# Turning the last batch's queries and keys by DMA, with half of the first folds on GpSimd and PSUM banks chosen by the plan

## Chip, cores and metric

One Trainium2 chip, one core. The metric is the device time of one launch in microseconds, the median of several runs. Line numbers (L351) are those of the kernel before in its profile.

## What is computed

Two layers after each other, for 4 batches, 8 heads of 64, 768 positions. First, attention in chunks of 32 queries: each chunk sees 16 keys to its left, its own 32, 8 to its right, and 8 memory keys. The heads side by side are `x` of 768 x 512. Then:

```
X = np.fft.fft(x, axis=1)
X = np.fft.fft(X, axis=2)
u = x + np.real(X)
mu, var = mean and variance of u over its last axis
un = (u - mu) / np.sqrt(var + 1e-06)
out = u + np.maximum(un @ w_ch1, 0.0) @ w_ch2       # 512 -> 2048 -> 512
```

## The kernel before

**Attention** works on pairs of heads, `n = 0..15`, four for each batch. GpSimd issues the loads of queries and keys (`e_load_qk`, L324), cast to bf16, with eight consecutive positions in a partition: `qs` and `ks` are 96 partitions x 2 heads x 512, three buffers each. TensorE turns them (`turn`, L351: 16 transposes for each tile into the PSUM bank `tr`), ScalarE copies the queries out (`e_qT`, L360) and puts the keys with their overlap into `kTb` (`e_kT`, L379; VectorE in batch 0). Twelve tiles of 64 queries against 128 keys follow in two groups: scores (`e_scores`, L392), exp (`e_exp`, L400), values (`e_values`, L416), and the division on VectorE (`e_norm`, L426 and L427) into `xsb`. The values are loaded by SyncE (`e_load_v`, L333 to L342).

**Fourier.** VectorE folds `xsb` by its symmetries (`e_zy`, `e_pq`, `e_ff`; in batch 0 `g_zy` L556 and `g_ff` L569 to L574, in halves `g` as the rows come). ScalarE and VectorE split each fold into two fp16 parts (`e_hi`, `e_lo`, `g_hi` L590, `g_lo` L594). TensorE multiplies with cosine and sine tables along the rows (`e_rows` L488, `g_row` L614, `g_rows` L627), ScalarE and VectorE split again (L500, L505), TensorE goes along the columns (`e_columns` L638). In batches 1 to 3 the second half of the rows is written to DRAM (GpSimd, L522), mirrored there (SyncE, L526 and L527) and loaded again (GpSimd, L531).

**MLP.** Statistics and centring (L652, L658), then the turn of `un`: on TensorE in batch 0, by DMA transposes on SyncE in the others (`e_flip`, L670). `e_ch1` (L698) and `e_relu` (L706) make `hT`, `e_ch2` (L713) and `e_osb` (L720) the output, in two halves of the positions for each batch. PSUM banks for these come from two pools, `acc` and `mlp`, two banks each.

**The order** on each engine is written out by a planner, `Plan`. Every task has an engine, a cost, what it comes after, tags it takes and gives (buffers and banks), a rank, and for a DMA `moved` (its time alone on the DMA engines) and `late` (what is added until it lands). `order` plays this forward and places on each engine the first task in rank that is ready. MLP tasks have the highest ranks and fill TensorE's gaps. On the chip each engine then takes its instructions in that order and waits for what is missing. `share` divides the DMA engines between the queues. On GpSimd a rank below that of the loads puts a task ahead of them. `behind` holds a task back until another has been issued. For some 33 us TensorE's gaps are filled with matmuls on zeros (`e_fill`, L771).

The loads of pair n stand behind those of pair n - 1, and the first pair of batch 1 behind a one-element copy (`gate`, L824) that waits for the values of the last pair of batch 0:

```
lq, lk = [add("POOL", 0.9, lambda i=i: e_load_qk(n, i), take=(("qs", "ks")[i],),
              moved=1.2, late=LATE if b else 0.0,
              behind=t_gate if n == HP else t_ck.get(n - 1), ...
```

Of the kernel before, what the change touches and what calls it, by code (L numbers as in the profile page):

```python
# [36 lines left out]
class Plan:  # L37
# [11 lines left out]
    def __init__(self, slots):  # L49
        self.free = dict(slots)  # L50
        self.tasks = []

    def add(self, engine, cost, emit, after=(), take=(), give=(), rank=None, moved=0.0,
            loose=False, late=0.0, filler=False, behind=None, lag=0.0):
# [3 lines left out]
                 late=late, filler=filler, behind=behind, lag=lag)  # L58
# [3 lines left out]
    def share(self, now):  # L62
# [3 lines left out]
        while any(left.values()):  # L66
            heads = [xs_[0] + [2.0 if q == "POOL" else 1.0] for q, xs_ in left.items() if xs_]
            live = [h for h in heads if h[2] <= at + 1e-9]
            whole = sum(h[3] for h in live)
            step = min([h[1] * whole / h[3] for h in live]  # L70
# [4 lines left out]
            for q, xs_ in left.items():  # L75
                if xs_ and xs_[0][2] <= at - step + 1e-9:
                    xs_[0][1] -= step * (2.0 if q == "POOL" else 1.0) / whole
# [12 lines left out]
    def order(self):  # L90
        now, idle = 0.0, {}
        self.flow, self.seen = {}, 0.0
        waiting = {}
# [6 lines left out]
        while any(waiting.values()):  # L100
            for tag in [g for g in gives if g[0] <= now]:
                gives.remove(tag)
                self.free[tag[1]] += 1
            moved = False
            for e, ts_ in waiting.items():
# [3 lines left out]
                for t in ts_:  # L109
# [12 lines left out]
                    for tag in t["take"]:  # L122
                        need[tag] = need.get(tag, 0) + 1
# [3 lines left out]
                    for tag in t["take"]:  # L127
                        self.free[tag] -= 1
                    cost = t["cost"] * (2.0 if e == "PE" and now < self.WARM else 1.0)
                    idle[e] = t["end"] = now + cost  # L130
                    if t["moved"]:
                        self.flow.setdefault(e, []).append([t, t["moved"], now + cost])
                        self.share(now)
                        t["end"] = t["done"]
                    else:
                        t["done"] = now + cost + self.LAG.get(e, 0.07)
                    for tag in t["give"]:
                        gives.append((t["done"], tag))
# [25 lines left out]
def kernel(  # L164
# [61 lines left out]
    NKT = 2  # L226
    kTb = [spool.tile([P, NT, P], BF16, name=f"kTb{i}") for i in range(NKT)]

    cp_q = "p h j d -> p h (j d)"
# [3 lines left out]
    plan = Plan(dict(qs=NS, ks=NS, va=NV, kTb=NKT, qT=2, tr=1, sc=1, xa=1, e1=3,  # L233
# [87 lines left out]
    def e_load_qk(n, i):  # L321
        b, pr = seq[n]
        src, dst = ((q, qs), (k, ks))[i]
        nc.gpsimd.dma_start(dst[n % NS][0:QP],  # L324
# [28 lines left out]

    def e_turn_q(n):
# [22 lines left out]
    def e_kT(n, eng=None):  # L377
        trk = tr_of.pop((n, 1))
# [6 lines left out]
    def e_scores(n, g):  # L385
        qT, kT = qT_of[n], kTb[n % NKT]
        sc_of[n, g] = sc = aps.tile([P, 2, 8, 64], FP32, tag="sc", bufs=1, name="sc")
        for t6 in range(6):
            t = 6 * g + t6
            for hh in range(2):  # L390
                r0 = 64 * hh
                nc.tensor.matmul(sc[:, hh, t6, :], kT[r0:r0 + 64, t, :],  # L392
                                 qT[r0:r0 + 64, ts(t, 64)], start=True, stop=True,
# [158 lines left out]
    def g_zy(par, g):  # L552
        if g == 0:
            zy_of[0, par] = fpool.tile([P, NST, P], FP32, tag="unT", bufs=2, name="zy0")
        xb, sl = xs[0], slice(3 * g, 3 * g + 3)
        nc.vector.tensor_tensor(zy_of[0, par][:, sl], xb[:, sl, 0:P], xb[:, sl, HD:HD + P],  # L556
                                ALU.add if par == 0 else ALU.subtract)

    def g_ff(par, ab, g, last):
# [3 lines left out]
        zy, ff = zy_of[0, par][:, sl], ff_of[0, par][:, ab, sl]  # L563
        plus = ab == par
        if last:
            plus = plus == (par == 0)
        if not last:
            if ab == 0:
                nc.vector.tensor_copy(ff[:, :, 0], zy[:, :, 0])  # L569
            elif par == 0:  # L570
                nc.vector.memset(ff[:, :, 0:1], 0.0)
        elif (par, ab) == (1, 1):
            nc.vector.tensor_tensor(ff[:, :, 0], xb[:, :, P], xb[:, :, HD + P], ALU.subtract)
        nc.vector.tensor_tensor(ff[:, :, 1:P], (ff if last else zy)[:, :, 1:P],  # L574
# [115 lines left out]
    def mtag(b, i):  # L690
        return "acc" if i % 3 == 2 else "mlp"
# [3 lines left out]
    def e_ch1(b, sh, ht):  # L695
        ph_of[b, sh, ht] = ph = bank(mtag(b, ht), [P, 512], FP32, "ph")
# [12 lines left out]
    def e_ch2(b, sh, stl, part):  # L709
        if part == 0:  # L710
            pc_of[b, sh, stl] = bank(mtag(b, stl), [P, DM], FP32, "pc")
# [95 lines left out]
    t_gate, LATE = None, 1.0  # L807

    def attention(n):
# [3 lines left out]
        lq, lk = [add("POOL", 0.9, lambda i=i: e_load_qk(n, i), take=(("qs", "ks")[i],),  # L813
                      moved=1.2, late=LATE if b else 0.0,
                      behind=t_gate if n == HP else t_ck.get(n - 1),
# [3 lines left out]
                 take=("va",), moved=2.7, late=LATE if b else 0.0)  # L819
        t_lv[n] = lv  # L820
        t_ck[n] = lk
        if n == HP - 1:
            def e_gate():
# [3 lines left out]
        tq = add("PE", 0.40, lambda: e_turn_q(n), [lq, t_idb], take=("tr",), give=("qs",))  # L827
        dve = ("DVE", nc.vector.tensor_copy) if n < HP else ("ACT", None)
        eq = add("ACT", 0.80, lambda: e_qT(n), [tq], take=("qT",), give=("tr",),
                 rank=SINES - 0.5 if n == 0 else None)  # L830
        ktag = "acc" if first else "tr"
        tk = add("PE", 0.43, lambda: e_turn_k(n), [lk, t_idb, t_kz if n == 0 else t_kzs], take=(ktag,), give=("ks",))
        mk = t_mk[n] = add("DVE", 0.2, lambda: e_mkT(n), [t_mkT, t_kTz[n % NKT], t_mk.get(n - 1)],
                           take=("kTb",))
        ek = add(dve[0], 1.25 if dve[1] else 1.04, lambda: e_kT(n, dve[1]), [tk, mk], give=(ktag,))
# [68 lines left out]
    def weights(n):  # L904
        if n == HP + 1:
            t_w1.extend(add("POOL", 0.7, lambda dt=dt: nc.gpsimd.dma_start(
                w1_sb[:, dt, :], moe_w_ch1[ts(dt, P), :]), moved=2.55,
                behind=t_ck[n], rank=t_ck[n]["rank"] + 0.1) for dt in range(NDT))
        else:
            t_w2.extend(add("POOL", 0.7, lambda g=g: nc.gpsimd.dma_start(  # L910
                w2_sb[:, ts(g, 4), :], w2v[:, ts(g, 4), :]), moved=3.1,
                behind=t_ck[n], rank=t_ck[n]["rank"] + 0.1) for g in range(4))

    def first_fourier():
        t_rest, t_mid, t_row, pre = {}, {}, {}, {}
        for g in range(2):
            for par in range(2):
                zy = add("DVE", 0.5, lambda par=par, g=g: g_zy(par, g),
                         [t_norm[0, g], t_norm[1, g], t_sines],
                         take=("unT",) if g == 0 else ())  # L920
                for ab in range(2):
                    pre[par, ab, g] = add("DVE", 0.62 if ab == 0 else 0.5,
                                          lambda par=par, ab=ab, g=g: g_ff(par, ab, g, 0),
                                          [zy, t_norm[2, g]],
# [34 lines left out]
    def fourier(b):  # L959
        t_x1 = add("POOL", 1.0, lambda: e_rows_out(b), [t_norm[b * HP + i, 1] for i in range(HP)],  # L960
                   moved=2.0)
        t_x2[b] = add("SP", 0.6, lambda: e_rows_turn(b), [t_x1], moved=5.5, loose=True)
# [172 lines left out]
```

## Time and profile before

| | us |
|---|---|
| runs | 294.01, 292.42, 291.95 |
| the profiled execution | 292.92 |
| its span | 291.2 |
| TensorE busy | 274.1 |
| VectorE, ScalarE busy | 164.8, 164.9 |
| GpSimd busy | 48.2 |
| L698 and L713, busy | 88.9, 88.0 |
| L416, busy | 25.9 and 3.6 |
| L351, busy | 9.3 and 9.1 |
| L392, busy | 11.4 |

The busy time of a line adds up the time in which any of its instructions was under way. TensorE's matmuls overlap, so the mean of one row (218 ns for L351) times its count is far more than its busy time. The sums of the last batch alone are read from the list in order of time, start to next start. Attention of batch 0 lies at 5 to 32 us, its Fourier part at 33 to 60, the last attention group of batch 3 at about 160, the last Fourier part at 185 to 210, and from there to 287 there are only MLP matmuls on TensorE.

### The profile page before, as it was taken

What the parts mean: (1) busy time and instruction counts of PE and PEld (TensorE: products, weight loads), DVE (VectorE), ACT (ScalarE), POOL (GpSimd) and SP (SyncE); (2) the same over time, 40 slices, a digit from 0 to 9 for tenths busy, and PEclk for the clock granted to TensorE, in tenths of its full rate; (3) what the DMA queues carried; (4) which work ended last, traced back from release to release, by engine and by line L of the source; (5) the groups of instructions that cost most, each with busy time, mean ns of one, the idle gap of its engine ahead of it and who ended that gap; (6) DMA issues with size and microseconds to landing.
All of it is one profiled execution on the core that took longest, in us unless ns stands there. A gap on an engine that the chain in (4) does not pass through costs nothing.

```text
span 291.2 us, 7349 instructions
## 1 busy us (share of the span) xinstructions
PE 274.1 (94%) x3055; PEld 172.7 (59%) x3055; DVE 164.8 (57%) x354; ACT 164.9 (57%) x294; POOL 48.2 (17%) x96
## 2 busy tenths in 40 slices
PE   1589998999999999999999999999899999999994
PEld 1366797765566766566677646656554644545541
DVE  7968997952259874948885878864912012012011
ACT  6896546777566586877885246433750721712700
POOL 8824832220321010221010021010020000000000
PEclk9999999999999999999999999999999999999998
DMA  6998999997999987799952356944222504004204
GB/s 106 194 192 152 201 212 197 197 198 145 174 193 279 173 203 131 102 138 210 184 69 90 37 140 187 146 145 110 54 54 74 108 2 125 21 36 107 39 36 108
DMA packets 98689, 38.36 MB, mean 132 GB/s; under 512 B 85728, under 2 KB 93920, under 8 KB 98656
## 3 DMA queue, kind: packets, MB, share of 16 engines
q1 hardware_dynamic: 87344, 21.83, 40.7%
q0 software_dynamic: 10592, 15.21, 28.4%
q10 hardware_dynamic: 720, 0.85, 0.9%
q8 instruction: 24, 0.39, 0.6%
q14 instruction: 9, 0.07, 0.1%
HBM read 37.36 MB, written 13.37 MB: 174 GB/s over the span
## 4 chain that ended last, share of the span: by engine, by line
PE 86%; POOL 4%; DVE 4%; DMA 2%; ACT 1%; issue 1%; POOLq 0%; DVEq 0%
PE pc L713 29%; PE ph L698 28%; PE xa L416 7%; PE ps L488 5%; PE pm L638 3%; PE sc L392 3%; DMA ks<-in_k_dram 2%; PE ps L627 2%; PE trk L351 2%; PE trq L351 2%; PE idle L771 2%; DVE st L652 1%; DVE xsb L644 1%; POOL qs L324 1%; PE xo L416 1%
## 5 line engine op out<-in xcount | busy, mean ns | idle before, releaser
L706 ACT ACTIVATE hT<-ph 128x384 f16<-128x384 f32 x128 | 60.8, 492 | 53.0 <-PE ph L698 52.0
L698 PE MATMUL ph<-unT,w_sb 128*128 128x384 f16 x512 | 88.9, 327 | 0.9 <-ACT hT L706 0.6
L713 PE MATMUL pc<-w_sb,hT 128*128 128x512 f16 x384 | 88.0, 380 | 0.0
L698 PEld LDWEIGHTS <-w_sb 128*128 128x128 f16 x512 | 48.3, 98 | 33.2 <-issue 1.8
L713 PEld LDWEIGHTS <-hT 128*128 128x128 f16 x384 | 35.8, 98 | 40.6 <-issue 0.4
L720 DVE SCALAR_TENSOR_TENSOR osb<-pc,rstd,xsb 128x512 f32<-128x512 f32 x24 | 18.0, 750 | 72.4 <-PE pc L713 69.7
L400 ACT ACTIVATE e<-sc,mbias 128x384 f32<-128x384 f32 x64 | 33.6, 578 | 11.8 <-PE sc L392 11.2
L416 PEld LDWEIGHTS xa<-va,e 128*64 128x64 f32 x672 | 21.9, 138 | 7.2 <-issue 5.7
L416 PE MATMUL xa<-va,e 128*64 128x65 f32 x672 | 25.9, 226 | 0.3 <-issue 0.3
L658 ACT ACTIVATE un<-xsb,mu_s 128x512 f16<-128x512 f32 x24 | 17.2, 722 | 14.2 <-DVE mu_s L653 14.2
L500 ACT CAST up<-ps 128x386 f16<-128x386 f32 x16 | 9.7, 604 | 16.9 <-PE ps L488 15.6
L652 DVE BATCH_NORM_STATS2 st<-xsb 128x6 f32<-128x512 f32 x24 | 16.6, 690 | 0.7
L324 POOL DMA_DIRECT2D qs<-in_q_dram x16 | 10.5, 659 | 35.3 <-PE trq L351 19.1
L427 DVE TENSOR_TENSOR xsb<-xa,zs 128x384 f32<-128x384 f32 x28 | 15.6, 558 | 1.0
L360 ACT COPY qT<-trq 128x768 bf16<-128x768 bf16 x16 | 12.7, 796 | 6.0 <-PE trq L351 6.0
L505 DVE TENSOR_TENSOR up<-ps,up 128x386 f16<-128x386 f32 x16 | 9.5, 594 | 10.5 <-ACT up L500 10.5
L426 DVE RECIPROCAL zs<-xa 128x6 f32<-128x6 f32 x28 | 5.3, 191 | 16.4 <-PE xa L416 16.0
L379 ACT COPY kTb<-trk 128x1056 bf16<-128x1056 bf16 x12 | 12.5, 1040 | 2.2 <-PE trk L351 2.2
L351 PE MATMUL trq<-ident_b,qs 96*64 96x96 bf16 x256 | 9.1, 218 | 4.9 <-DMA qs<-in_q_dram 4.9
L324 POOL DMA_DIRECT2D ks<-in_k_dram x16 | 10.2, 638 | 20.7 <-PE trk L351 16.9
L644 DVE TENSOR_TENSOR xsb<-pm,xsb 128x512 f32<-128x512 f32 x15 | 10.1, 670 | 5.4 <-PE pm L638 5.4
L351 PE MATMUL trk<-turn_b,ks 100*64 100x100 bf16 x256 | 9.3, 220 | 3.9 <-DMA ks<-in_k_dram 2.9
(142 smaller groups left out, 329.2 us busy)
## 6 DMA issues: line engine op xcount, KB each, us to landing
va<-in_v_dram SPq DMA_DIRECT2D x32, 220.0 KB
w_sb<-in_moe_w_ch_dram POOLq DMA_DIRECT2D x8, 512.0 KB, 16.6
qs<-in_q_dram POOLq DMA_DIRECT2D x16, 192.0 KB, 5.7
ks<-in_k_dram POOLq DMA_DIRECT2D x16, 192.0 KB, 6.9
out_dram<-osb SPq DMA_DIRECT2D x12, 256.0 KB
x_rows<-xsb POOLq DMA_DIRECT2D x3, 768.0 KB, 4.9
xr<-x_back POOLq DMA_DIRECT2D x3, 768.0 KB, 5.6
out_rows<-osb SPq DMA_DIRECT2D x9, 256.0 KB
```

Source lines behind the costliest of these rows:

```text
L324: nc.gpsimd.dma_start(dst[n % NS][0:QP], src[b, 2 * pr:2 * pr + 2].rearrange("h (p j) d -> p h (j d)", j=RB))
L351: nc.tensor.transpose(out_[64 * hh:64 * hh + 64, j * w:(j + 1) * w], src[:, hh, j * D:(j + 1) * D], eye)
L400: nc.scalar.activation(e1[:, :, :, ts(half, 32)], sc[:, :, 0:6, ts(half, 32)], AFT.Exp, bias=mbias[:, half:half + 1], scale=1.0 / math.sqr ...
L416: nc.tensor.matmul(xa[64 * half:64 * half + 64, st, hh, 0:65], e1[:, hh, t6, :], v1[:, hh, 6 * g + t6, 0:65], start=True, stop=True)
L427: nc.vector.tensor_tensor(xs[b][:, 3 * g:3 * g + 3, 2 * pr * D:(2 * pr + 2) * D] .rearrange("p s (h d) -> p s h d", h=2), xa[:, :, :, 0:D] ...
L488: nc.tensor.matmul(out_[:, sp, :], part[:, ab, sp * 3 + st, c0:c1], tab[:, sp, st, :], start=(st == 0 and i == 0), stop=(st == 2 and i == 1))
L652: nc.vector.bn_stats(st6, xs[b][:, kt, :])
L658: nc.scalar.activation(un, xs[b][:, kt, :], AFT.Identity, bias=mu_of[b][:, kt, 0:1], scale=-1.0)
L698: nc.tensor.matmul(ph[:, 0:384], w1_sb[:, dt, ts(ht, P)], unT_of[b][:, dt, sh * 384:(sh + 1) * 384], start=(dt == 0), stop=(dt == NDT - 1))
L706: nc.scalar.activation(hT_of[b, sh][:, ht, :], ph[:, 0:384], AFT.Relu, bias=0.0, scale=-1.0)
L713: nc.tensor.matmul(pc_of[b, sh, stl], hT_of[b, sh][:, ht, ts(stl, P)], w2_sb[:, ht, :], start=(ht == 0), stop=(ht == NHT - 1))
L720: nc.vector.scalar_tensor_tensor(osb, pc, rstd_of[b][:, st:st + 1], xs[b][:, st, :], ALU.mult, ALU.add)
```

## The change

For pairs of the last batch (`b >= TURNED`, which is 3) the load puts both heads of a position side by side, as two DMAs of 768 runs of 64 elements for each tile. Two DMA transposes on SyncE turn the tile: the queries into `qT` (128 x 8 x 96: positions j of each run of eight outermost), the keys into a new buffer `kU` (two of them, 128 x 8 x 128, set to zero once by GpSimd). ScalarE copies from `kU` to `kTb` as before from PSUM. The scores read the queries in eight runs of eight and write PSUM with a step of eight elements, so that the result lies as before. The turns on TensorE and the copy `e_qT` fall away for these pairs.

```diff
+    KR, KS, NKU = 16, 128, 2
+    kU = [spool.tile([P, RB, KS], BF16, name=f"kU{i}") for i in range(NKU)]
+    TURNED = 3
...
     def e_load_qk(n, i):
+        if b >= TURNED:
+            for hh in range(2):
+                nc.gpsimd.dma_start(
+                    dst[n % NS][0:QP].rearrange("p h (j d) -> p (h j) d", d=D)[:, hh::2],
+                    src[b, 2 * pr + hh].rearrange("(p j) d -> p j d", j=RB))
+            return
...
+    def e_flip_q(n):
+        qT_of[n] = qT = apool.tile([P, RB, QP], BF16, tag="qT", bufs=2, name="qT")
+        nc.sync.dma_start_transpose(qT, qs[n % NS].rearrange("p h c -> p (h c)"))
+
+    def e_flip_k(n):
+        nc.sync.dma_start_transpose(kU[n % NKU][:, :, KR:KR + QP],
+                                    ks[n % NS][0:QP].rearrange("p h c -> p (h c)"))
...
     def e_kT(n, eng=None):
+        if n >= TURNED * HP:
+            nc.scalar.copy(
+                strided(kTb[n % NKT], MEM0 + NMEM, [[P, NT], [RB, 11], [1, RB]]),
+                strided(kU[n % NKU], KR - KOFF, [[64 // RB, NT], [1, 11], [KS, RB]]))
+            return
...
-                nc.tensor.matmul(sc[:, hh, t6, :], kT[r0:r0 + 64, t, :],
-                                 qT[r0:r0 + 64, ts(t, 64)], start=True, stop=True,
+                if n < TURNED * HP:
+                    own, to = qT[r0:r0 + 64, ts(t, 64)], sc[:, hh, t6, :]
+                else:
+                    own = strided(qT[r0:r0 + 64], t * 64 // RB, [[QP, RB], [1, 64 // RB]])
+                    to = strided(sc[:, hh, t6, :], 0, [[1, RB], [RB, 64 // RB]])
+                nc.tensor.matmul(to, kT[r0:r0 + 64, t, :], own, start=True, stop=True,
```

Batch 0's early folds of the second half (`g == 1`) move from VectorE to GpSimd:

```diff
     def g_zy(par, g):
+        xb, sl, eng = xs[0], slice(3 * g, 3 * g + 3), nc.gpsimd if g == 1 else nc.vector
...
     def g_ff(par, ab, g, last):
+        eng = nc.gpsimd if g == 1 and not last else nc.vector
```

The planner gets `pick`: an MLP task takes a bank of either pool, the one that has been free longest. And it gets other weights and due times for the DMAs:

```diff
-    def mtag(b, i):
-        return "acc" if i % 3 == 2 else "mlp"
+    pick_of = {}
+
+    def pick(*key):
+        return pick_of.setdefault(key, dict(of=("mlp", "acc")))
...
-            heads = [xs_[0] + [2.0 if q == "POOL" else 1.0] for q, xs_ in left.items() if xs_]
+            heads = [xs_[0] + [xs_[0][0]["grain"], q] for q, xs_ in left.items() if xs_]
...
+    t_uz = add("POOL", 0.4, lambda: [nc.gpsimd.memset(kU[i], 0.0) for i in range(NKU)], rank=20)
...
-        lq, lk = [add("POOL", 0.9, lambda i=i: e_load_qk(n, i), take=(("qs", "ks")[i],),
-                      moved=1.2, late=LATE if b else 0.0,
-                      behind=t_gate if n == HP else t_ck.get(n - 1),
+        lq, lk = [add("POOL", 1.6 if b >= TURNED else 0.9, lambda i=i: e_load_qk(n, i),
+                      take=(("qs", "ks")[i],), moved=3.1 if b >= TURNED else 1.2, grain=0.032 if b >= TURNED else 0.1, late=LATE if b else 0.0,
+                      behind=t_gate if n == HP else t_xr[b - 2] if n == TURNED * HP else t_ck.get(n - 1),
...
+        if b >= TURNED:
+            eq = add("SP", 1.2, lambda: e_flip_q(n), [lq], take=("qT",), give=("qs",),
+                     late=5.0, loose=True, behind=t_flip[0])
+            t_flip[0] = tk = add("SP", 1.2, lambda: e_flip_k(n), [lk, t_uz], take=("kU",),
+                                 give=("ks",), late=5.0, loose=True, behind=eq)
+            ek = add("ACT", 2.05, lambda: e_kT(n), [tk, mk], give=("kU",))
...
-                zy = add("DVE", 0.5, lambda par=par, g=g: g_zy(par, g),
+                early = ("DVE", "POOL")[g]
+                zy = add(early, (0.5, 1.1)[g], lambda par=par, g=g: g_zy(par, g),
                          [t_norm[0, g], t_norm[1, g], t_sines],
-                         take=("unT",) if g == 0 else ())
+                         take=("unT",) if g == 0 else (), rank=20.1 if g else None)
...
-                t_un[kt] = add("SP", 0.1, lambda kt=kt: e_flip(b, kt),
-                               [un, t_un.get(kts[i - 1]) if i else None],
-                               take=("unT",) if i == 0 else (), give=("un",), moved=0.8,
+                t_un[kt] = add("SP", 1.2, lambda kt=kt: e_flip(b, kt),
+                               [un], behind=t_un.get(kts[i - 1]) if i else None,
+                               take=("unT",) if i == 0 else (), give=("un",), late=2.5,
                                loose=True)
```

The figures of values' loads, weights, mirrored rows and outputs (`moved`, `grain`, `late`) change in the same manner. For the values, `late` is 4.0 in batch 1 instead of 1.0. Since all engines' orders come from one plan, these figures can move any task.

## Prediction

> **What bounds the kernel now.** I read the page first, then the busy time by stretch, then TensorE's instructions in order, then waits and the queues of SyncE and GpSimd. The page's share of busy time and the slices:
>
> ```profile
> span 291.2 us, 7349 instructions
> ...
> PE 274.1 (94%) x3055; PEld 172.7 (59%) x3055; DVE 164.8 (57%) x354; ACT 164.9 (57%) x294; POOL 48.2 (17%) x96
> ...
> PE   1589998999999999999999999999899999999994
> ```
>
> An average of 94% does not say where the other 6% lies. By stretch (columns: us, busy time of each engine with its instructions, TensorE clock, DMA share, GB/s):
>
> ```profile
> 0.00:20.00 20.00, 9.83 (x195) 7.08 (x196) 16.48 (x52) 15.69 (x22) 14.12 (x43) 1.00 1.03 161
> ...
> 100.00:120.00 20.00, 20.00 (x238) 13.38 (x237) 13.23 (x27) 15.11 (x27) 2.07 (x3) 1.00 0.76 142
> 120.00:140.00 20.00, 20.00 (x357) 12.50 (x354) 14.59 (x33) 16.07 (x28) 3.71 (x5) 1.00 1.04 169
> ...
> 200.00:220.00 20.00, 19.11 (x117) 10.94 (x115) 10.00 (x23) 10.80 (x22) 1.60 (x2) 1.00 0.27 63
> ```
>
> From 60 to 200 us TensorE has no gap; later only 0.9 us at 206 to 209. A busy matmul row could hide a slow pipeline, so I took the pace from the chain of waits: 24 L698 matmuls in 4.01 us at 102 us and 64 in 10.40 at the end (167 and 163 ns), 16 of L713 in 3.56 at 123 and 48 in 10.36 at the end (223 and 216). It is real work at nearly the same pace. The gaps are 10.2 us before 20 us, small ones up to 55, and the tail. Hence the rule for this sum: after about 33 us a microsecond of TensorE work removed is a microsecond of span, and work moved among the other engines is worth nothing unless TensorE comes to wait for it. Of TensorE's waits for data there is little:
>
> ```profile
> PE trq L351 <- DMA qs<-in_q_dram: 4.9, 2, 4.2
> PE trk L351 <- DMA ks<-in_k_dram: 2.9, 2, 2.5
> ```
>
> The first two are the cold start (the largest at 5.8 and 9.1 us). The instructions the change replaces, with what follows them in TensorE's order (start us, us):
>
> ```profile
> 132.79 0.35 PE L392 MATMUL sc<-qT,kTb 64*128 64x64 bf16 x12
> 133.06 0.55 PE L351 MATMUL trk<-turn_b,ks 100*64 100x100 bf16 x16
> 133.54 0.82 PE L698 MATMUL ph<-unT,w_sb 128*128 128x384 f16 x4
> ...
> 136.83 0.53 PE L351 MATMUL trq<-ident_b,qs 96*64 96x96 bf16 x16
> 137.29 0.50 PE L698 MATMUL ph<-unT,w_sb 128*128 128x384 f16 x2
> ```
>
> The reader should take start to next start as the cost: 0.48 us for keys, 0.46 for queries, 0.27 for twelve score matmuls. For one more edit, the start on GpSimd and the TensorE row that hangs on it:
>
> ```profile
> 9.32 1.99 POOL L754 MEMSET ks<- 4x1024 bf16 x2
> ...
> 15.21 0.65 POOL L324 DMA_DIRECT2D qs<-in_q_dram  x1
> 15.85 0.63 POOL L324 DMA_DIRECT2D ks<-in_k_dram  x1
> ```
>
> ```profile
> 22.43 0.54 PE L351 MATMUL trk<-turn_b,ks 100*64 100x100 bf16 x16 [0.42 <-DMA ks<-in_k_dram]
> ```
>
> **What the Trainium skill says.** "PSUM — Partial Sum Buffer", Specifications: PSUM lines hold 8 bytes and a non-contiguous pattern slows matmuls significantly. The new scores write PSUM with a step of eight fp32. Every output of the trace before is contiguous, so no row here shows it. "SBUF — State Buffer", Door 1: lines of 16 bytes, no loss while accesses stay in one. A run of eight bf16 is one line, so I cost the new query read at nothing; it says the opposite of ScalarE's read of the turned keys, with a step of 128 elements; no run shows either. The same page, Who interferes with whom: a GpSimd operation that reads SBUF and a VectorE one with two SBUF inputs exclude each other. The trace before has no long such pair. "DMA: Bandwidth & Descriptors", Issuing engines are not separate DMA queues: transfers from all queues run on the same engines. The stretches agree: the DMA share is about 1 while loads from both queues are out.
>
> **The change part by part.**
>
> *Turns removed.* The last batch has four head pairs, a query and a key turn each (128 matmuls). By start to next start: queries at 119.84, 126.45, 130.50, 136.83: 0.47 + 0.37 + 0.47 + 0.46 = 1.77; keys at 122.42, 127.93, 133.06, 148.30: 0.47 + 0.48 + 0.48 + 0.38 = 1.81. All on the path: **-3.6 us**.
>
> *Scores.* Eight groups of twelve matmuls, now reading runs of eight and writing with a step. Today two matmuls (one per head) start together every 29 ns or so for 64 columns: bound by columns. If writes run at half rate, each of six pairs costs some 26 ns more: 0.15 us a group, 1.2 in all. At a quarter rate it is 0.47 a group, 3.7 in all. Nothing at best. I take half rate because a PSUM line holds two fp32 and the step wastes one: **+1.2 us**, ends 0 and 3.7.
>
> *ScalarE.* Four qT copies of 0.80 us fall away (-3.2). The four key copies read SBUF with a step instead of PSUM: 1.04 us now; the plan books 2.05; so 0 to +4.0. Between -3.2 and +0.8 in a stretch where ScalarE works 15 to 16 of 20 us: hidden by its spare 4 us in 20 and by the MLP matmuls that TensorE has in between. 0.
>
> *Loads of queries and keys.* One issue of 192 runs becomes two of 768 short ones each: GpSimd's 0.63 us per issue becomes two issues per tensor, 1.3 to 1.6, so some 6 to 8 us more on GpSimd over the batch, which works 3.7 of 20 us there. On the DMA engines: queue 1 moves packets of about 250 bytes at 40.7% of 16 x 291.2 us / 87,344 = 21.7 ns; 1536 of them over 16 engines are 2.1 us a tensor. Queue 0's packets now take 28.4% of 16 x 291.2 / 10,592 = 125 ns, so 192 are 1.5 us. +0.6 each by that; twice the packet price would make it +2.7: 5 to 22 us of DMA time for eight tensors. The first two pairs were issued at 83 to 92 us and must now wait for the issue of the mirrored rows of batch 1 (103.5 us); their queries were turned at 119.8, so 16 us are left against a median landing of 5.7. Hidden, if the plan keeps its distance.
>
> *Transposes on SyncE.* Eight are added. The trace has their like:
>
> ```profile
> 163.44 4.87 SPq L670 DMA_TRANSPOSE unT<-un  x3
> ```
>
> One issue of 128 x 512 takes 1.2 us of SyncE, then the data moves within about a microsecond (the DMA share is 0.63 and 0.68 at 206 to 208 us after an issue at 204.67). The new ones are 96 x 1024, 1.5 times the elements: 1.2 to 2.4 us each, 10 to 19 us of SyncE over the batch. Each waits at the head of SyncE's queue for its load; behind it stand the values' loads of the next pairs and the mirrored rows of batch 2 (L526, L527), for which the matmuls L416 and GpSimd's L531 wait. L531 of that batch is issued at 150.6 and its data used from about 163: 10 us of room. The plan counts 1.2 + 5.0 us until a transpose is usable; I expect 3 to 5. 0 on the path in the likeliest case; the upper end is in the rivals.
>
> *Start.* Three edits. (a) The memset of both kU buffers on GpSimd has rank 20 and no condition, so it goes ahead of the fourth pair's loads at 15.21. The row with the same 1024 bf16 elements gives 2.0 us for two (the plan books 0.4). The key turn of that pair at 22.43 waits for this load, and score matmuls are queued behind it: 0 if the order leaves room, +2.0 if not. (b) Half of the first folds moves from VectorE to GpSimd: two L556 (0.5) and four L574 (0.5): 3 us off VectorE, which is full from 32 to 44 us. But TensorE runs its row matmuls without a gap from 33.2 to 44.6 and only then waits once, 0.85 us at 45.4 for ScalarE: at most -0.85. (c) Against it, GpSimd and VectorE can block each other there, and GpSimd's own queue holds the loads of the second batch and the small sums L600 that the first row matmul waits for: up to +1. I take 0 for the three together, with ends -0.85 and +3.
>
> *Banks chosen at run of the plan.* The MLP matmuls may now take either pool of PSUM banks. TensorE waited 0.6 us for L706 in the whole kernel, so there is nothing to win: 0, in the noise either way. New DMA weights and due times alter the order everywhere and no amount of work.
>
> *Sum.* -3.6 + 1.2 + 0 = **-2.4 us** against the span of 291.2. The profiled execution was reported as 292.92; the other runs have 291.95 to 294.01, median 292.42. I take the difference over unchanged: **290.0 us**. A measurement of this kernel can tell about 1% (2.9 us) from no change, so the likeliest case is itself near the edge of what shows.
>
> **The rivals.**
>
> 1. *Free writes, and the start wins.* If stepped PSUM writes cost nothing and VectorE's relief takes out the wait at 45.4: 292.42 - 3.6 - 0.85 = 288.0. For it: a paired matmul writes 64 columns to two banks, so the two streams need not meet. Against it: the skill's sentence on PSUM.
> 2. *The turns come back as slow scores.* At a quarter rate: 292.42 - 3.6 + 3.7 = 292.5. For it: nothing in the kernel before writes this way, so nothing excludes it. Against: half a line is used, not a quarter.
> 3. *SyncE's head of line; this is the slower side.* A query transpose waits at the head of SyncE's queue for a load that lands late, the values' loads behind it are late too, and TensorE, which takes its instructions in order, stands before the scores with all the MLP work queued behind. For it: landings of key loads range from 3.5 to 18.6 us with a median of 6.9, the DMA share is near 1 from 104 to 112 and from 124 to 148 us, and the edit adds DMA time there. Against: the plan books long delays, and TensorE's order then has MLP work before the scores. Price: each microsecond by which the worst transpose is later than planned is one of TensorE. With 6 us late (a landing of 13 instead of 7) the time is 292.42 - 2.4 + 6 = 296.0. It is slower than before from 2.4 us late on, and by over 1% from 5.3.
> 4. *It does not free TensorE.* If batch 3 came so late that its MLP waited, the gap would fall in at the end. Batch 3's last flip is issued at 215.5 and its MLP starts at about 249, so it needs over 30 us of delay; I give it no chance of its own.
>
> **How the numbers follow.** Likeliest case 0.48, its own range 288.6 to 291.8 (scores from nothing to 3.0); rival 1 0.18; rival 2, with start losses of about 2 us added to the likeliest, 0.16; rival 3 0.18. Below 289.5 lie most of rival 1 (0.17) and a third of the likeliest (0.16): 0.33. Above 295.3 lies rival 3 from 5.3 us late on, about 0.6 of it, with a little for two losses together (0.15 in all). The rest, 0.52, is within 1%. The range that leaves out no more than 2 in 10 goes from 287.8 (rival 1) to 295.0 (rival 3 up to 5 us late).
>
> **What would show each step.** No L351 rows after about 95 us, and 384 of them instead of 512. The last batch's score matmuls one pair every 53 ns or so (right), 29 (rival 1) or 107 (rival 2). Stepped ScalarE copies of the keys between 1.0 and 2.1 us. TensorE at 20.00 of 20 from 60 to 200 us still; a wait of TensorE's scores for a DMA or ScalarE's key copy, or of the values for a load, is rival 3. The start shows in the time at which TensorE begins L627 or L614, 33.4 us now. I am wrong if TensorE's work after 33 us falls by something other than 2.4 us, or if a stretch after 60 us has gaps.

## The result, and the profile after

The changed kernel takes 291.13 us (median of five runs, 290.92 to 291.56), the kernel before, measured beside it, 293.01 (291.95 to 294.01): a ratio of 0.994, interval 0.991 to 0.997. That is 0.6% faster, inside the 1% that the prediction called no change; the forecast was 290.0. The profiled executions have spans of 289.2 and 291.2 us.

The page of the changed kernel first. Line numbers moved: the turn is L374, the scores L433, the key copies L410 (new) and L415, the rows L655 and L668, the MLP L741 and L756.

```profile
span 289.2 us, 7127 instructions
...
PE 272.9 (94%) x2932; PEld 170.5 (59%) x2932; DVE 166.0 (57%) x345; ACT 167.7 (58%) x290; POOL 65.1 (23%) x115
...
PE   1588989999999999999999999999999999999994
```

TensorE has 123 instructions and 1.2 us of busy time less, GpSimd 17 us more (the folds, the short loads). The slice of 8 around 206 us is a 9 now. Busy time by stretch, in the columns used before:

```profile
20.00:40.00 20.00, 17.65 (x330) 13.21 (x328) 17.27 (x36) 11.43 (x20) 13.15 (x21) 1.00 1.00 171
40.00:60.00 20.00, 19.80 (x305) 15.92 (x304) 18.13 (x42) 12.89 (x22) 8.73 (x14) 1.00 1.09 198
100.00:120.00 20.00, 20.00 (x258) 13.91 (x257) 15.44 (x35) 15.19 (x27) 10.00 (x13) 1.00 1.61 179
120.00:140.00 20.00, 20.00 (x238) 11.41 (x238) 14.70 (x31) 12.28 (x20) 5.52 (x7) 1.00 1.37 200
...
200.00:220.00 20.00, 20.00 (x128) 11.91 (x127) 10.90 (x24) 10.70 (x21) 1.59 (x2) 1.00 0.24 53
```

TensorE is full from 60 us to the tail. The first part of the last batch's attention, up to 140 us, now runs at a DMA share of 1.4 to 1.6, and nothing on TensorE waits for it. TensorE's waits for data are nearly all at the start:

```profile
PE trq L374 <- DMA qs<-in_q_dram: 5.1, 2, 4.1
...
PE trk L374 <- DMA ks<-in_k_dram: 1.3, 2, 1.0
...
PE ps L668 <- DVE hl L635: 1.0, 1, 1.0
```

The groups with the new operations (count, then busy us and mean ns of one):

```profile
L433 PE MATMUL sc<-qT,kTb 64*128 64x64 bf16 x384 | 12.6, 205 | 0.5 <-ACT e L440 0.5
L410 ACT COPY kTb<-kU 128x1056 bf16<-128x1056 bf16 x4 | 8.2, 2059 | 1.5 <-DMA kU<-ks 1.5
L415 ACT COPY kTb<-trk 128x1056 bf16<-128x1056 bf16 x8 | 8.3, 1038 | 0.6 <-PE trk L374 0.6
L374 PE MATMUL trk<-turn_b,ks 100*64 100x100 bf16 x192 | 7.2, 223 | 2.1 <-DMA ks<-in_k_dram 1.3 <-POOL va L313 0.7
```

384 turns are left, 192 of each kind, as the change says.

Where did the time go? I summed TensorE's instructions from start to next start, in one profiled execution of each kernel:

| TensorE, us | before | after | difference |
|---|---|---|---|
| turns | 16.05 | 12.71 | -3.34 |
| scores | 9.23 | 10.41 | +1.18 |
| idle, and matmuls on zeros, before 60 us | 18.98 | 20.22 | +1.24 |
| gaps after 60 us | 0.89 | 0.00 | -0.89 |
| sum of these | | | -1.81 |
| end of the last matmul | 286.97 | 285.21 | -1.76 |

The other rows moved by up to 0.5 us either way and cancel. These terms are not good to a tenth of a microsecond, because executions differ. The kernels of two experiments below, the plain scores and the step on the read side, have the same order of instructions on TensorE, VectorE, ScalarE and GpSimd as the changed one. Where it shows 20.22 us of idle time and zeros before 60 us, they show 18.92 and 19.31; where it shows 12.71 us of turns, they show 13.11 and 13.02. Nearly all of this spread lies before TensorE's first row matmul of batch 0 (L655, at 34.07 us in the change), in the cold start. "The first row" below means this one.

### The profile page after: what moved, and what is told of

It is laid out like the page before. It is cut to its first block, busy times and chain, and to the rows that moved or that the text cites. A ratio compares the mean times of both kernels' runs of the same rounds, so it can differ in the third digit from the quotient of the medians.

```text
span 289.2 us, 7127 instructions
## 1 busy us (share of the span) xinstructions
PE 272.9 (94%) x2932; PEld 170.5 (59%) x2932; DVE 166.0 (57%) x345; ACT 167.7 (58%) x290; POOL 65.1 (23%) x115
## 4 chain that ended last, share of the span: by engine, by line
PE 85%; DVE 6%; POOL 5%; DMA 2%; issue 2%; ACT 0%; POOLq 0%
PE pc L756 29%; PE ph L741 29%; PE xa L456 7%; PE ps L528 5%; PE pm L679 5%; PE sc L433 3%; DMA ks<-in_k_dram 2%; PE trk L374 1%; DVE ff L615 1%; PE trq L374 1%; POOL qs L347 1%; DVE hl L635 1%; DVE up L545 1%; DVE xsb L467 1%; PE pm L579 1%
## 5 line engine op out<-in xcount | busy, mean ns | idle before, releaser
L749 ACT ACTIVATE hT<-ph 128x384 f16<-128x384 f32 x128 | 61.9, 491 | 50.6 <-PE ph L741 49.8
L741 PE MATMUL ph<-unT,w_sb 128*128 128x384 f16 x512 | 88.1, 326 | 0.0
L756 PE MATMUL pc<-w_sb,hT 128*128 128x512 f16 x384 | 87.8, 380 | 0.0
L741 PEld LDWEIGHTS <-w_sb 128*128 128x128 f16 x512 | 48.6, 98 | 32.0 <-issue 0.4
L756 PEld LDWEIGHTS <-hT 128*128 128x128 f16 x384 | 35.9, 98 | 41.0 <-issue 0.4
L440 ACT ACTIVATE e<-sc,mbias 128x384 f32<-128x384 f32 x64 | 33.6, 577 | 18.8 <-PE sc L433 18.8
L518 DVE TENSOR_TENSOR lo<-ff,hi 128x768 f16<-128x768 f32 x12 | 11.4, 954 | 4.7 <-ACT hi L513 4.7
L433 PE MATMUL sc<-qT,kTb 64*128 64x64 bf16 x384 | 12.6, 205 | 0.5 <-ACT e L440 0.5
L433 PEld LDWEIGHTS <-kTb 64*128 64x128 bf16 x384 | 8.5, 100 | 7.3 <-issue 6.1
L571 POOL DMA_DIRECT2D xr<-x_back x3 | 2.3, 778 | 44.3 <-DMA x_back<-x_rows 44.3
L513 ACT CAST hi<-ff 128x768 f16<-128x768 f32 x12 | 9.9, 827 | 3.3 <-DVE ff L505 3.0
L374 PE MATMUL trq<-ident_b,qs 96*64 96x96 bf16 x192 | 7.0, 220 | 5.1 <-DMA qs<-in_q_dram 5.1
```

Of the source, the lines that this page charges most:

```text
L433: nc.tensor.matmul(to, kT[r0:r0 + 64, t, :], own, start=True, stop=True, tile_position=(r0, 0))
L440: nc.scalar.activation(e1[:, :, :, ts(half, 32)], sc[:, :, 0:6, ts(half, 32)], AFT.Exp, bias=mbias[:, half:half + 1], scale=1.0 / math.sqr ...
L741: nc.tensor.matmul(ph[:, 0:384], w1_sb[:, dt, ts(ht, P)], unT_of[b][:, dt, sh * 384:(sh + 1) * 384], start=(dt == 0), stop=(dt == NDT - 1))
L749: nc.scalar.activation(hT_of[b, sh][:, ht, :], ph[:, 0:384], AFT.Relu, bias=0.0, scale=-1.0)
L756: nc.tensor.matmul(pc_of[b, sh, stl], hT_of[b, sh][:, ht, ts(stl, P)], w2_sb[:, ht, :], start=(ht == 0), stop=(ht == NHT - 1))
```

## The experiments

**Theory A** is the prediction's accounting: TensorE's own work decides, so the turns are worth what they take on TensorE, the stepped score writes cost 1.2 us on the path, and what other engines and the DMAs do is hidden. **Theory B** is that the gain comes from elsewhere (the new plan, the banks), or that the transposes' landing decides. Each kernel is the changed one with the edit shown; ratios are to the kernel before, measured beside it on the same chip.

### Turning on TensorE again

```diff
-    TURNED = 3
+    TURNED = 4
```

> All of the change but the turning by DMA: no batch is turned by DMA (TURNED is 4), so the last batch goes through TensorE's transposes and contiguous scores again; folds on GpSimd, banks, due times and the memset of kU stay. Theory A, the change is a sum of TensorE work (turns -3.6 us, scores +1.3): this loses the gain, 293.4 us (292.8 to 294.0), with TensorE busy without a gap from 60 us on. Theory B, the gain comes from the new order, the banks and the folds: 291.1 us (290.6 to 291.7), as with the whole change.

Measured: 293.86 us, ratio 1.002 (1.000 to 1.003). The rest of the change, without the turning, gains nothing; against the changed kernel's ratio the turning is worth some 0.75%, 2.2 us. Theory A. This kernel too has no gap after 60 us, so closing the one at 206 us belongs to the plan's other edits; which of them wasn't separated.

### Scores without the step in PSUM

```diff
-                    own = strided(qT[r0:r0 + 64], t * 64 // RB, [[QP, RB], [1, 64 // RB]])
-                    to = strided(sc[:, hh, t6, :], 0, [[1, RB], [RB, 64 // RB]])
+                    own = strided(qT[r0:r0 + 64], t * 64, [[1, 64]])
+                    to = sc[:, hh, t6, :]
```

> The whole change, but the last batch's scores read 64 neighbouring columns and write 64 neighbouring elements, so they take the wrong queries: the output of batch 3 is not the reference's, all instructions and sizes stay. Theory A: the groups of twelve go back from 0.44 to 0.28 us, eight of them give 1.28 us, 289.85 us (289.5 to 290.3). Theory B, the scores do not lie on the path: 291.1 us, with the 1.28 us found as a gap of TensorE.

Measured: 289.91 us, ratio 0.988 (0.984 to 0.992). A group of twelve takes 0.28 us by start to next start, 0.44 in the changed kernel, whose pairs follow every 56 ns instead of 29. A group and what follows it, first here, then in the changed kernel:

```profile
132.01 0.35 PE L433 MATMUL sc<-qT,kTb 64*128 64x64 bf16 x12
132.29 2.12 PE L741 MATMUL ph<-unT,w_sb 128*128 128x384 f16 x12
```

```profile
139.74 0.51 PE L433 MATMUL sc<-qT,kTb 64*128 64x64 bf16 x12
140.19 4.72 PE L741 MATMUL ph<-unT,w_sb 128*128 128x384 f16 x28
```

Eight groups are 1.3 us, and by the medians 1.2 us come back. The next experiment makes the same reading from a larger difference.

### The step on the read side

```diff
-                    own = strided(qT[r0:r0 + 64], t * 64 // RB, [[QP, RB], [1, 64 // RB]])
-                    to = strided(sc[:, hh, t6, :], 0, [[1, RB], [RB, 64 // RB]])
+                    own = strided(qT[r0:r0 + 64], t * 64 // RB, [[1, 64 // RB], [QP, RB]])
+                    to = sc[:, hh, t6, :]
```

> The whole change with the last batch's scores the other way round: the queries are read with a step of 96 elements, each in another line, and PSUM is written contiguously; the same result. Theory A with the cost in the PSUM writes and reads by step [...] (half rate): a pair of matmuls 53 to 58 ns and 291.1 us (290.7 to 291.6). If a stepped read runs at a quarter of the rate: 107 ns a pair, +2.4 us, 293.5 us. If stepped reads cost nothing: 29 ns a pair, 289.85 us.

Measured: 293.58 us, ratio 1.001 (0.999 to 1.003); a group takes 0.75 us. In the list of TensorE's instructions one of its groups reads:

```profile
131.59 0.82 PE L433 MATMUL sc<-qT,kTb 64*128 64x64 bf16 x12
```

The column after the start is busy time, with the drain of the last pair: 0.82 us here, 0.35 without a step. Reading bf16 with a step of 192 bytes runs at about a quarter of the rate, writing fp32 to PSUM with a step of 32 bytes at half: the changed kernel has the cheaper of the two places. Against the plain scores, eight groups are 3.8 us longer by their starts, and the kernel is 3.7 us slower by the medians: what the scores take on TensorE lies on the path. And reading in runs of eight costs nothing: the experiment with the exp, below, has such reads at 0.28 us a group.

### All the first folds on VectorE

```diff
-        xb, sl, eng = xs[0], slice(3 * g, 3 * g + 3), nc.gpsimd if g == 1 else nc.vector
+        xb, sl, eng = xs[0], slice(3 * g, 3 * g + 3), nc.vector
...
-        eng = nc.gpsimd if g == 1 and not last else nc.vector
+        eng = nc.vector
```

The planner's costs and ranks of these tasks go back with it.

> The whole change with the early folds of the second half of batch 0 on VectorE again, at their old costs and ranks. Theory A, the folds on GpSimd delay the first row matmuls (TensorE ends its rows of batch 0 at 46.3 us with the change and at 44.4 before): 290.3 us (289.8 to 290.8), the end of the rows near 44.5 us. Theory B, taking 3 us off VectorE is a part of the gain: 292.0 us (291.5 to 292.6).

Measured: 297.3 us (295.23 to 299.0), ratio 1.015 (1.010 to 1.019). Neither expectation. Idle time and matmuls on zeros before 60 us fell from 20.22 to 18.38 us, but only 0.5 of these 1.8 us lie after TensorE's first row; the rest is cold start, where executions of one order differ by 1.2. Meanwhile the plan's other order opened gaps of 3.04 us after 60 us. The longest of them in this kernel's list in order of time, and then stretches of 1 us (third from the right: TensorE's clock):

```profile
127.40 2.04 ACT L410 COPY kTb<-kU 128x1056 bf16<-128x1056 bf16 x1 [3.69 <-DMA kU<-ks]
...
129.49 0.51 PE L433 MATMUL sc<-qT,kTb 64*128 64x64 bf16 x12 [1.83 <-ACT kTb L410]
...
129.93 3.27 PE L756 MATMUL pc<-w_sb,hT 128*128 128x512 f16 x8
```

```profile
128.00:129.00 1.00, 0.00 (x0) 0.00 (x0) 1.00 (x2) 1.00 (x1) 1.00 (x2) 1.00 0.15 23
129.00:130.00 1.00, 0.51 (x13) 0.41 (x14) 0.52 (x1) 0.43 (x1) 1.00 (x2) 1.00 1.29 263
130.00:131.00 1.00, 1.00 (x4) 0.43 (x5) 0.00 (x0) 0.90 (x2) 0.30 (x1) 0.65 2.01 200
131.00:132.00 1.00, 1.00 (x4) 0.32 (x3) 0.47 (x1) 0.15 (x1) 0.00 (x0) 0.50 1.94 217
```

ScalarE stands 3.69 us before the key copy for the transpose (issued at 120.91, so 6.5 us before the copy could start), TensorE 1.83 us before the scores for the copy. Then the clock is at half for some 3 us, and eight L756 take 3.27 us where the eight before took 1.90. The Trainium skill, "TensorE: Matmul & The Clock Gate", Part 1, describes such halves of the clock after an idle window of about 3.4 us. The half is there; here a wait of 1.83 us came before it, shorter than that window; the trace decides, and 1.83 us was enough here. This is rival 3's kind of loss, with ScalarE at its head. The landing itself was hardly late: 6.5 us against the 6.2 that the plan books. ScalarE came to the copy 2.8 us after the issue. Two more kernels tested whether the loss hangs on the transposes.

### The same, with the transposes planned to land later

```diff
-                     late=5.0, loose=True, behind=t_flip[0])
+                     late=8.0, loose=True, behind=t_flip[0])
```

in both transposes, on top of the last edit. The plan then books 9.2 us from issue to use.

> The kernel with the folds back on VectorE (297.3 us, with TensorE waiting at 128 us for a key copy and through it for a DMA transpose, its clock down to 0.79 there) and one figure changed: the plan adds 8.0 instead of 5.0 us until a transpose has landed. Theory A, that kernel's loss is a transpose that lands later than the plan thinks: no wait of TensorE's scores, clock 1.00 in all stretches from 60 us, 290.6 us (290.0 to 291.3), since the folds on VectorE end the rows 0.9 us sooner. Theory B, VectorE's fuller queue is what costs: it stays above 294 us.

Measured: 294.59 us (291.98 to 298.51), ratio 1.005 (1.003 to 1.007). By the medians a more cautious due time won back 2.7 of the 6.2 us that the folds' edit had lost, and not all: the expected 290.6 was missed. In the profiled execution (291.98, its fastest) ScalarE still stands before key copies, and behind the second of these two the MLP's relus queue:

```profile
126.40 2.06 ACT L410 COPY kTb<-kU 128x1056 bf16<-128x1056 bf16 x1 [4.93 <-DMA kU<-ks]
...
138.99 1.99 ACT L410 COPY kTb<-kU 128x1056 bf16<-128x1056 bf16 x1 [3.03 <-DMA kU<-ks]
140.89 1.87 ACT L749 ACTIVATE hT<-ph 128x384 f16<-128x384 f32 x4
141.42 0.81 PE L741 MATMUL ph<-unT,w_sb 128*128 128x384 f16 x4 [1.93 <-ACT hT L749]
```

The first copy started 6.1 us after its transpose was issued (120.27), well inside the 9.2 us, and ScalarE stood 4.93 us for it all the same. It had come to the copy 1.2 us after the issue. So a transpose that lands later than planned is not what fails here. The kernel's 6.5 us of spread between runs fit an order that hangs on when transfers land; that this is what spreads them was not shown.

### The folds on VectorE without the turning

The folds' edit with `TURNED = 4`.

> The kernel with the folds back on VectorE (297.3 us) and no turning by DMA (TURNED is 4): banks, due times and the memset of kU are all that is left of the change. Theory C, that kernel's loss comes from transposes that land late in the order which its plan happens to give: without them no gap of TensorE from 60 us on and 292.5 us (291.9 to 293.3), about one us under the run without turning whose folds are on GpSimd. Theory B, VectorE's folds do not go with the new banks and due times: still above 295 us.

Measured: 293.19 us (291.91 to 296.19), ratio 1.000 (0.997 to 1.003): by its time case C of its expectation. The loss of the folds' edit needs the transposes. Idle time and zeros before 60 us are 17.84 us here against 19.66 with the folds on GpSimd and no turning. That the pair with turning (20.22 and 18.38) also differs by 1.8 us is no proof that the folds cost that much: after TensorE's first row the two pairs differ by 0.4 and 0.5 us, and the rest is cold start. Case C said no gap after 60 us, and there it missed: one of 1.4 us opens, the values' matmul waiting for a load.

### The change with the transposes planned to land sooner

```diff
-                     late=5.0, loose=True, behind=t_flip[0])
+                     late=2.0, loose=True, behind=t_flip[0])
```

in both, the folds as in the change.

> The whole change with one figure changed: the plan adds 2.0 instead of 5.0 us until a transpose has landed. Theory A, the late due time is a needed part of the change: TensorE's scores of the last batch wait for key copies, each first wait up to 3 us, 294 to 299 us. Theory B, a DMA of this size lands in time anyway, the 5.0 is only caution: 291.1 us (290.5 to 291.7).

Measured: 293.0 us (292.09 to 296.16), ratio 1.001 (0.999 to 1.003). 1.9 us slower than the change, in the direction of theory A's line and less than it said. The profiled execution has one gap, in the stretch that was full:

```profile
120.00:140.00 20.00, 18.80 (x241) 10.76 (x238) 13.25 (x30) 12.95 (x20) 5.52 (x7) 1.00 1.32 199
```

TensorE waits 1.2 us there for an exp (L440), on the engine that stood 2.05 and 2.45 us before its key copies.

### The step moved into ScalarE's exp

```diff
-                    to = strided(sc[:, hh, t6, :], 0, [[1, RB], [RB, 64 // RB]])
+                    to = sc[:, hh, t6, :]
...
     def e_exp(n, g):
+        if n >= TURNED * HP:
+            for half in range(2):
+                for hh in range(2):
+                    nc.scalar.activation(
+                        e1[:, hh, :, ts(half, 32)],
+                        strided(sc[:, hh], 4 * half, [[64, 6], [1, 4], [RB, RB]]),
+                        AFT.Exp, bias=mbias[:, half:half + 1], scale=1.0 / math.sqrt(D))
+            return
```

> The whole change, but the last batch's scores write PSUM contiguously in the order of the turned queries, and the exp on ScalarE reads PSUM with the step and puts them into order: four instructions of 128 x 192 for each group instead of two of 128 x 384 (the plan's cost 1.6 instead of 1.12). Theory A: groups of twelve at 0.28 us, 1.28 us of TensorE saved; ScalarE's stepped reads of PSUM are as fast as contiguous ones (the key copy before reads bf16 there with a step at 0.98 ns an element), about 0.4 us each, hidden: 289.9 us (289.4 to 290.5). Theory B, the longer exp puts TensorE to waiting: 291.5 us or more.

Measured: 290.19 us (289.6 to 291.15), ratio 0.991 (0.988 to 0.993). The scores' groups are back at 0.28 us while they still read runs of eight, so those are free. ScalarE pays in its own time:

```profile
L448 ACT ACTIVATE e<-sc,mbias 128x384 f32<-128x384 f32 x48 | 25.2, 578 | 12.8 <-PE sc L433 12.4 <-POOL va L315 0.4
...
L442 ACT ACTIVATE e<-sc,mbias 128x192 f32<-128x192 f32 x32 | 10.9, 425 | 5.7 <-PE sc L433 5.7
```

Four of 425 ns for two of 578: 0.54 us a group, 4.4 over eight, in an engine with room, and no gap after 60 us. It is faster than the kernel before. The changed one, measured at another time, is 0.9 us slower by the medians; five of the six runs here lie below all of its runs, but the intervals of the two ratios overlap.

### Two batches turned by DMA

```diff
-    TURNED = 3
+    TURNED = 2
...
-                      behind=t_gate if n == HP else t_xr[b - 2] if n == TURNED * HP else t_ck.get(n - 1),
+                      behind=t_gate if n == HP else t_xr[1] if n == 3 * HP else t_ck.get(n - 1),
```

> The dose doubled: batches 2 and 3 both turned by DMA (TURNED is 2; the rows of batch 1 still hold back the loads of batch 3). Theory A, a sum of TensorE work: four more pairs, -3.6 + 1.3 = -2.3 us, 288.8 us (288.2 to 289.6). Theory B, the DMA engines, full up to 112 us, cannot take the short runs of four more pairs: transposes or values land late and TensorE waits, 293 us or more.

Measured: 318.23 us (313.96 to 319.47), ratio 1.080 (1.074 to 1.086). Theory B, rival 3 in full. TensorE's longest waits and two stretches:

```profile
PE sc L433 <- ACT kTb L410: 9.9, 1, 9.9
PE ph L741 <- DMA unT<-un: 6.9, 1, 6.9
```

```profile
120.00:140.00 20.00, 9.01 (x132) 5.53 (x131) 10.62 (x26) 7.51 (x12) 9.16 (x12) 0.76 1.72 158
140.00:160.00 20.00, 12.79 (x106) 8.10 (x106) 6.98 (x13) 7.12 (x15) 2.43 (x3) 0.64 0.92 177
```

The short loads land after 10 us in the median (7.5 and 6.6 in the change). One key transpose issued at 124.39 kept SyncE 4.74 us, the key copy started 11.7 us after its issue, and the values' loads stood behind it on SyncE until 129.18. TensorE's clock (third column from the right) was at half for 23.9 us from 130.3 on, which comes on top of 20.7 us of gaps. The turns on TensorE did fall by another 3.4 us (12.71 to 9.29).

### The memset behind the loads

```diff
-    t_uz = add("POOL", 0.4, lambda: [nc.gpsimd.memset(kU[i], 0.0) for i in range(NKU)], rank=20)
+    t_uz = add("POOL", 0.4, lambda: [nc.gpsimd.memset(kU[i], 0.0) for i in range(NKU)], rank=100000)
```

> The whole change, with the memset of the two kU buffers behind the fourth pair's loads on GpSimd; nearly all other instructions keep their order. If the delay of 1.9 us of these loads lies on the path, TensorE's wait of 1.0 us for the fourth key tile goes: 290.4 us (289.9 to 290.9). If the cold start hides it: 291.1 us (290.7 to 291.6).

Measured: 291.03 us, ratio 0.992 (0.989 to 0.995): as the change. The 1.0 us wait for the fourth key tile is gone. In its place TensorE waits before its first rows for GpSimd, which it does not in the change:

```profile
PE ps L655 <- POOL mid L643: 0.7, 1, 0.7
```

Idle time and zeros before 60 us are 20.53 us here and 20.22 in the change.

### The last two good edits together

The exp with the step, and the memset behind the loads.

> Contiguous scores with the reordering in the exp (290.2 us) together with the memset behind the fourth pair's loads. If the two add up: 289.5 us (289.0 to 290.0), the fastest so far. If the start hides the memset: 290.2 us. If the new order lets a transpose land late: 292 us or more, with a gap of TensorE at 120 to 160 us.

Measured: 289.89 us (289.69 to 292.33), ratio 0.990 (0.987 to 0.994), faster than the kernel before and 0.4% under the change by the ratios. Its interval overlaps the change's and covers that of the exp alone, so the memset's part can't be told.

## Why the prediction was right, and where it was off

The mechanism was right, and the size nearly: -1.9 us by the medians (-2.0 by the spans) against -2.4. A part of that nearness is luck: two terms that I took as 0 came to +1.24 and -0.89 us and nearly cancel.

- **Turns removed.** Said -3.6, measured -3.34. The 128 turns are gone. From TensorE's first row on the term is -3.53 (10.55 to 7.02 us); the rest is cold start, in which the same number of turns takes 5.5 to 6.3 us from one kernel to the next. For the same reason the kernel without the turning shows 16.84 us for its 512 turns instead of 16.05: from the first row on it has 10.66.
- **Scores.** Said +1.2 from half-rate writes, measured +1.18 in the sums and 1.2 by taking the step out. The Trainium skill, "PSUM — Partial Sum Buffer", Specifications, says that such writes slow a matmul significantly; the runs say to about half the rate, for a step of eight fp32. Rivals 1 (free) and 2 (a quarter) fall: pairs every 56 ns, where 53, 29 and 107 were to tell them apart. A quarter is what the read with a step costs.
- **ScalarE, 0.** The key copies take 2.06 us, the upper end of 1.04 to 2.05. It stayed hidden: no gap after 60 us, as said.
- **Loads and transposes, 0.** Two issues a tensor at 0.78 us, within the 1.3 to 1.6 said. Seven of the eight transposes keep SyncE 1.2 to 1.3 us and one 1.8, together 10.5 us, the lower end. Of the landing I expected 3 to 5 us; the one on which ScalarE waited shows 4.95, between these two lines of the list in order of time:

```profile
120.91 1.32 SPq L382 DMA_TRANSPOSE kU<-ks  x1
...
125.86 2.05 ACT L410 COPY kTb<-kU 128x1056 bf16<-128x1056 bf16 x1 [1.45 <-DMA kU<-ks]
```

  So of the plan's 6.2 us some 1.2 were left as a margin, the small end of what I expected. Rival 3 didn't come in the change, but it was near: ScalarE stands 1.45 us there and 3.69 in the folds' kernel. And it works otherwise than I said. I argued a load that lands late at SyncE's head of line; in all four kernels that show such a gap, ScalarE stands before the key copy, with exps and relus behind. SyncE's order has its part in how late the transpose comes, but not by its load: the first key tile's load had landed at 112.1 us in the change and at 113.3 in the folds' kernel, and its transpose was issued at 120.91 in both, behind other issues. In the folds' kernel the landing was 0.3 us over the plan's figure, so my price, a microsecond for each microsecond of late landing, doesn't hold there.
- **Start, taken as 0** from ends of -0.85 and +3. This is the term of the sum that is off by most: +1.24 in the table. But 0.99 of it lies before TensorE's first row (17.89 us before, 18.88 in the change), where the two kernels with the change's order show 17.70 and 18.06; so it can't be put down to an edit. From the first row to 60 us it is +0.26 (1.08 to 1.34). (a) The memset's 2 us reach one wait and no further: without it there is a wait before the first rows instead. That is 0, as taken. (b) The relief came in full: the wait of 0.85 us at 45.4 us is gone in all nine kernels with the folds on GpSimd and stands in the four with all of them on VectorE. (c) The block came too, and took the relief back. The list in order of time shows how. Before, two low parts of a fold took VectorE 1.02 us:

```profile
35.02 1.02 DVE L594 TENSOR_TENSOR hl<-ff,hl 128x384 f16<-128x384 f32 x2
```

After, the same two stand beside GpSimd's fold, and TensorE's row matmuls behind them:

```profile
37.15 2.57 POOL L615 TENSOR_TENSOR ff<-zy,xsb 128x381 f32<-128x381 f32 x2
...
37.53 2.61 DVE L635 TENSOR_TENSOR hl<-ff,hl 128x384 f16<-128x384 f32 x2
...
38.93 0.51 PE L668 MATMUL ps<-cosS,hl 128*128 128x193 f16 x4 [1.01 <-DVE hl L635]
```

  The Trainium skill, "SBUF — State Buffer", Who interferes with whom, says that a GpSimd operation that reads SBUF and a VectorE one with two SBUF inputs contend; the trace agrees, at 2.6 times the duration, and at 42.47 us in the same trace two such low parts without a fold of GpSimd beside them take 1.02 us again. TensorE's wait of 0.9 to 1.0 us for this row stands in all nine kernels with the folds on GpSimd and in none of the other four. So 0 for (b) and (c) was near because two effects of about a microsecond cancel. And in the whole kernel the folds' return gave nothing (293.19 against 293.86 without the turning, with overlapping runs) or lost, while the plan's later order changed with it.
- **Banks, 0.** The gap of 0.89 us at 206 us closed, and does so without the turning. I had read the 0.6 us for L706 as noise; some edit of the plan won it, and I can't say which.

What stays open: why ScalarE comes to the key copies so soon after the issue in the two folds' kernels, also with the later due time, and whether a plan with better-kept figures could have both the folds' start and the turning. The plan's clock and the chip's may part by some microseconds before batch 3, so that a margin in the plan is not a margin on the chip; that is argued, not shown.

## What to carry to other kernels

Where one engine is full, price a change by that engine's start-to-next-start times, operation by operation; here that gave the scores and the turns to 0.1 us, once the cold start is set apart. Put an awkward step where there is slack: on the engine that evacuates PSUM it cost nothing that shows, in the bounding matmul a half or three quarters of its rate. Work moved to a DMA is free only by the margin between landing and use on every in-order queue that stands before it, so read that margin from the trace and count the copy's engine among these queues.

## What the hardware showed that I had not expected

- Stepped PSUM writes and stepped reads differ: the twelve start in pairs every 56 ns with the step in PSUM, every 110 with the step in the reads, every 29 or 30 with neither.
- ScalarE's copy of 1056 bf16 takes 2.06 us from SBUF with a step of 256 bytes (L410), 1.04 from PSUM (L415); its exp of 192 fp32 from PSUM with a step 0.425 us, against 0.578 for 384 in order.
- DMA transposes of 96 x 1024 keep SyncE 1.2 us at least, like those of 128 x 512 that were there before; some took more, up to 2.6 us in the kernels with one batch and 4.7 with two; they were usable 3.8 to 6.5 us after issue in the kernels with one batch, 11.7 with two.
- The clock fell to half after a wait of 1.83 us in one kernel and not after one of 1.93 in another, so a gap's price can be more than its length; what decides between the two was not found.
